# One-bank PSUM tiles for gate and up in the second token half of a fused attention and gated MLP kernel

## The chip, the cores and the metric

The kernel runs on one core of a Trainium2 chip. The metric is the device time of one launch in microseconds (us). The engines are named as in the profile: PE (TensorE, matmuls; PEld is its weight loads), DVE (VectorE), ACT (ScalarE), POOL (GpSimd) and SP (SyncE, which issues most transfers here).

## What is computed

The reference is a transformer block with adaptive layer norm: attention of 2048 tokens with 32 query heads over the last 512 cached keys, and then a gated MLP. The change touches the MLP only:

```
h = _layernorm(x) * (1 + cb) + sb          # [2048, 576]
gate = h @ W_gate                          # [2048, 4608]
up   = h @ W_up
gate = gate * (gate > 0)
x = x + gb * ((gate * up) @ W_down)        # [2048, 576]
```

All inputs are float32. The kernel splits a matmul operand into a high and a low part (`hi`, `lo`) and adds three products: hi with hi, hi with lo, lo with hi.

## The kernel before

**Order of the work.** On PE, DVE, ACT and POOL the instructions run in the order in which the program issues them; only SP's queue is ordered by the framework. Attention comes first (`NU` units), then the MLP, written as a generator (`mlp_slots`, L1412) that issues one *slot* at each step.

**Passes.** The MLP has 36 passes `m`. `m // NFP` (`NFP` = 18) is the token half, 1024 tokens as two blocks of 512, and `m % NFP` picks two of the 36 tiles of 128 features. A pass computes gate and up of a 2 x 2 block (two feature tiles by two token blocks) with seven products in place of eight, a scheme of Strassen's kind: `order` (L767) gives P1, P6, P2, P7, P5, P4, P3, and sums of the products make the four results. Passes 0 to 17 are the first token half, 18 to 35 the second.

**A slot** is one product. `prod` (L1034) runs 7 matmuls for the gate half (`xx` = 0) and 7 for the up half (`xx` = 1), each into 128 x 512 float32. P2 and P3 go on adding in the PSUM that P1 and P5 filled; the other five products get new PSUM from `new_pair` (L1147). In the second token half `evac_half` (L1098) is issued after each half: for gate it is one DVE instruction (L1074, L1076, L1110 or L1115, by product), for up one or two (L1079 adds into PSUM, L1080 multiplies the clipped gate with up; L1110; L1115, after which ACT copies the up half at L1117). P1 is the exception: nothing after the gate half, and one ACT copy of both halves (L1104) after the up half. Results are cut into hi and lo by ACT and POOL (`h_out`, `fast_split`).

**Pieces of the down projection** of pass m - 1 are put between the halves. An ordinary piece (`md_piece`, L647) is 12 matmuls into 128 x 576, which DVE adds to `acc` (L601). The passes in `FAST` (18 to 33) do the down projection too with seven products in place of eight: `fast_piece` (L659), 14 pieces of 6 matmuls, one in each half of the next pass's slots. Their sums are added to `acc` by DVE (L673, L679); in the first such pass, which starts the accumulators anew, eight of them are copied by ACT (L677). The weights for these pieces are made by POOL and ACT (`fast_weights`, L698), and operands by `fast_later` (L1082) and `fast_last` (L1092).

**PSUM.** A tile `[P, 2, 512]` float32 is a pair of banks, one for gate and one for up. The pool `psS` has two pairs, `psW` one; from the start of the MLP `psX` has one more, in the place of attention's `psM`. Gate and up take turns in three pairs, two of `psS` and the one of `psX`, by the list `free`: `new_banks` (L1142) takes its first entry, and L1446 puts a pair back when its last product is issued. All pieces use the one pair of `psW` (L584, L665), but for the last eight (L1450), of which every second one uses `psS`. The framework makes an instruction wait for earlier users of its tile.

**Loads.** `w_prep` (L828) loads the weights of the product two slots on (`wop`, 640 KB); it is called by `others` (L1404).

Of the kernel before, what the change touches and what calls it, by code (L numbers as in the profile page):

```python
# [7 lines left out]
F32 = mybir.dt.float32  # L8
# [3 lines left out]
ALU = mybir.AluOpType  # L12
AX = mybir.AxisListType

P = 128
# [16 lines left out]
def kernel(  # L32
# [13 lines left out]
    nc = tc.nc  # L46
# [11 lines left out]
    op = ctx.enter_context(tc.tile_pool(name="op", bufs=3))  # L58
    xp = ctx.enter_context(tc.tile_pool(name="xp", bufs=3))
    sp = ctx.enter_context(tc.tile_pool(name="sp", bufs=2))  # L60
    psS = ctx.enter_context(tc.tile_pool(name="psS", bufs=2, space=bass.MemoryType.PSUM))
    psW = ctx.enter_context(tc.tile_pool(name="psW", bufs=1, space=bass.MemoryType.PSUM))
    psM_scope = tc.tile_pool(name="psM", bufs=2, space=bass.MemoryType.PSUM)
    psM = psM_scope.__enter__()
# [576 lines left out]
    NFP = NFT // 2  # L641
    NB = 2 * NFP
    ds_, hhi, hlo = {}, {}, {}
    wop, wraw, hop = {}, {}, {}
    pair, tmp = {}, {}

    def md_piece(m, k, qt, pool=None):  # L647
        b, fp = divmod(m, NFP)
        i = 8 * b + 4 * k + qt
        down_piece([hhi[m, f, k] for f in range(2)], [hlo[m, f, k] for f in range(2)],  # L650
                   [ds_[m, f] for f in range(2)], i, qt, f"md{m}_{k}_{qt}", pool=pool)()
        if fp == NFP - 1:
            nc.sync.dma_start(out[i * P:(i + 1) * P, :], acc[i])


    FAST = range(NFP, NB - 2)
    fop, fw = {}, {}

    def fast_piece(m, kind, n):  # L659
        if kind == "4":  # L660
            specs = [(fop[m, "A22"], fw[m, "4"], 0, 2 * n + j) for j in range(2)]
        else:
            a, b = {"16": ("A11", "S2"), "75": ("S3", "S1"), "23": ("A12", "S4")}[kind]
            specs = [(fop[m, x], fw[m, kind], j * H2, n) for j, x in enumerate((a, b))]
        ps = psW.tile([P, 2, 512], F32, tag="w", name=f"mf{m}_{kind}_{n}")  # L665
        for j, ((hi, lo), (whi, wlo), c, qt) in enumerate(specs):
            sl = slice(qt * P, (qt + 1) * P)
            for i, (x, w) in enumerate(((hi, whi), (hi, wlo), (lo, whi))):
                nc.tensor.matmul(ps[:, j, :H2], x[:, sl], w[:, c:c + H2], start=i == 0, stop=i == 2)  # L669
        if kind == "4":  # L670
            for j in range(2):
                a = acc[8 + 2 * n + j][:, :H2]
                nc.vector.tensor_tensor(a, ps[:, j, :H2], a, op=ALU.add)  # L673
            return
        a = acc[{"16": 0, "75": 4, "23": 12}[kind] + n].rearrange("p (h n) -> p h n", h=2)
        if kind != "23" and m == FAST[0]:
            nc.scalar.copy(a, ps[:, :, :H2])  # L677
        else:
            nc.vector.tensor_tensor(a, ps[:, :, :H2], a, op=ALU.add)  # L679
# [87 lines left out]
    def order(m):  # L767
        return ("P1", "P6", "P2", "P7", "P5", "P4", "P3")
# [265 lines left out]
    def prod(m, s, n, xx):  # L1034

        hs, w = hop[m // NFP, OPS[s][1]], wop[n]
        ps = pair[m, s][:, xx, :]
        ops = []
        for t in range(2):
            ops += [(w[:, xx, t, :], hs[t]), (w[:, xx, 3 + t, :], hs[t]), (w[:, xx, t, :], hs[3 + t])]  # L1040
        ops.append((w[0:96, xx, 2, :], hs[2][0:96]))
        for i, (a, c) in enumerate(ops):
            nc.tensor.matmul(ps, a, c, start=s not in ("P2", "P3") and i == 0, stop=i == len(ops) - 1,  # L1043
                             skip_group_check=True)
# [26 lines left out]
    def gated_half(x, ps, r, a, op1=ALU.add):  # L1071
        if x == 0:
            if a is None:
                nc.vector.tensor_scalar(r, ps[:, 0, :], 0.0, None, op0=ALU.max)  # L1074
            else:
                nc.vector.tensor_tensor(r, ps[:, 0, :], a[:, 0, :], op=ALU.add)  # L1076
            return
        if a is not None:
            nc.vector.tensor_tensor(ps[:, 1, :], ps[:, 1, :], a[:, 1, :], op=op1)  # L1079
        nc.vector.scalar_tensor_tensor(r, r, 0.0, ps[:, 1, :], op0=ALU.max, op1=ALU.mult)  # L1080

    def fast_later(m):  # L1082
        r21, s1 = tmp[m, "r"][:, 0, :], tmp[m, "r"][:, 1, :]
# [8 lines left out]
    def fast_last(m):  # L1092
        r12, s4 = tmp[m, "q"][:, 0, :], tmp[m, "q"][:, 1, :]
        fast_split(m, "A12", r12)
        nc.gpsimd.tensor_sub(s4, r12, tmp[m, "c"][:, 1, :])
        fast_split(m, "S4", s4)

    def evac_half(m, s, x):  # L1098
        ps, fast = pair[m, s], m in FAST
        if s == "P1":  # L1100
            if x == 0:
                tmp[m, "q"] = pp.tile([P, 2, 512], F32, tag="hi", name=f"q{m}")
            else:
                nc.scalar.copy(tmp[m, "q"], ps)  # L1104
                if m - 1 in FAST:
                    fast_last(m - 1)
            return
        q = tmp[m, "q"]
        if s == "P6":
            nc.vector.tensor_tensor(q[:, x, :], ps[:, x, :], q[:, x, :], op=ALU.add)  # L1110
            return
        if s == "P7":
            if x == 0:
                tmp[m, "r"] = pp.tile([P, 2, 512], F32, tag="lo", name=f"r{m}", bufs=2)
            nc.vector.tensor_tensor(tmp[m, "r"][:, x, :], ps[:, x, :], q[:, x, :], op=ALU.add)  # L1115
            if x:
                nc.scalar.copy(q[:, 1, :], ps[:, 1, :])  # L1117
            return
        if s == "P2" and x == 0:
            tmp[m, "r22"] = xp.tile([P, 640], F32, tag="xm", name=f"r{m}")[:, :512]  # L1120
        if s == "P5" and x == 0:
            tmp[m, "c"] = pp.tile([P, 2, 512], F32, tag="lo", name=f"c22_{m}", bufs=2)
        f, k, r, a, op1 = {"P2": lambda: (0, 0, tmp[m, "r22"], None, ALU.add),
                           "P5": lambda: (1, 1, tmp[m, "c"][:, 0, :], tmp[m, "r"], ALU.add),
                           "P4": lambda: (1, 0, tmp[m, "r"][:, 0, :], tmp[m, "r"], ALU.add),
                           "P3": lambda: (0, 1, q[:, 0, :], q, ALU.subtract)}[s]()
        gated_half(x, ps, r, a, op1)
        if x == 0:
            return
        if not fast:  # L1130
            h_out(m, f, k, r)
        elif s == "P2":
            fast_split(m, "A22", r)
        elif s == "P5":
            fast_split(m, "A11", r)
        elif s == "P4":
            fast_later(m)


    npair, px, free, kind = [0], {}, ["s", "s"], {}  # L1140

    def new_banks(nm):  # L1142
        npair[0] += 1
        k = free.pop(0)
        return (px["x"] if k == "x" else psS).tile([P, 2, 512], F32, tag=k, name=nm), k

    def new_pair(m, s):  # L1147
        pair[m, s], kind[m, s] = new_banks(f"gu{npair[0]}")

    def evac(m, s):  # L1150
        ps = pair[m, s]
# [169 lines left out]
    for i in range(1, len(VIS)):  # L1321
        g, qbs = VIS[i]
# [40 lines left out]
    for i, ab in enumerate(lay0 + lay):  # L1363
        n = i - len(lay0) - 2 * NFT + 4
# [21 lines left out]
    for i in range(4):  # L1386
        m = 2 + 2 * i
# [23 lines left out]

    def mlp_slots():  # L1412
        for m in range(NB):
            md = [lambda k=k, qt=qt: md_piece(m - 1, k, qt) for k in range(2) for qt in range(4)] if m else []
            if m - 1 in FAST:
                md = fast_pieces(m - 1)
            for i, s in enumerate(order(m)):
                flush_stores()
                if s not in ("P2", "P3"):
                    new_pair(m, s)  # L1420
                else:
                    pair[m, s], kind[m, s] = (x[m, {"P2": "P1", "P3": "P5"}[s]] for x in (pair, kind))
                prod(m, s, 7 * m + i, 0)
                if m or i:
                    sums(m, i)
                    others(m, i)
                if m >= NFP:
                    evac_half(m, s, 0)
                if m and i or m - 1 in FAST:
                    md.pop(0)()  # L1430
                elif filler and not m:
                    filler.pop(0)()
                for fn in mextra.pop((m, i - 1, True), []):
                    fn()
                prod(m, s, 7 * m + i, 1)
                wop.pop(7 * m + i)
                if m >= NFP:
                    evac_half(m, s, 1)
                if m and i < 2 or m - 1 in FAST:
                    md.pop(0)()  # L1440
                elif filler and not i:
                    filler.pop(0)()
                if m < NFP:
                    evac(m, s)
                if s not in ("P1", "P5"):
                    free.append(kind[m, s])  # L1446
                yield
        for k in range(2):
            for qt in range(4):
                md_piece(NB - 1, k, qt, (psS, "s") if qt % 2 else None)  # L1450
        flush_stores()
        assert not mextra and not filler

# [202 lines left out]
```

## Time and profile before

| | us |
|---|---|
| median of 3 runs | 2997.86 (2995.13 to 2999.44) |
| the profiled execution | 2994.6 |
| its span, first to last instruction | 2992.5 |
| MLP, first token half: about | 1667 to 2323 |
| pass 18: about | 2323 to 2360 |
| pass 19 | 2360.55 to 2404.29 |
| passes 20 to 34 | 2404.29 to 2939.31 |
| pass 35 | 2939.31 to 2975.55 |
| the last eight pieces | 2975.55 to the end |

The page has the busy time of each engine, the chain of work that ended last, and the costliest groups of instructions. A row of a group reads: line, engine, operation, what is written from what, shape, count, then busy us and the mean ns of one, then the engine's idle time before them and who ended it. In the table of windows the columns are: the stretch, its length, busy us (and instructions) of PE, PEld, DVE, ACT and POOL, the granted TensorE clock, the DMA share, GB/s. In the list of waits the columns are us in total, times, longest us. A row in order of time gives the start, the duration, engine, line, what is done, the count of merged instructions, and in brackets the idle time before and its releaser.

### The profile page before, as it was taken

How to read it: one execution, taken by the hardware profiler on the slowest of the kernel's cores; microseconds unless marked ns; L12 is line 12 of the kernel's file. 1: busy time of each engine (PE TensorE's matmuls, PEld its weight loads, DVE VectorE, ACT ScalarE, POOL GpSimd, SP SyncE). 2: the span in 40 equal slices, each digit the busy share in tenths (PEclk: the TensorE clock that was granted, in tenths of full speed). 3: DMA queues.
4: the chain of work that ended last, by engine and by line, in shares of the span. 5: the costliest groups of instructions: out<-in, count | busy, mean ns of one | idle time of the engine just before them, and what ended most of it. 6: DMA issues, size and time to landing. Idle time of an engine off the chain costs nothing.

```text
span 2992.5 us, 41535 instructions
## 1 busy us (share of the span) xinstructions
PE 2900.6 (97%) x15256; PEld 2496.2 (83%) x15256; DVE 2189.5 (73%) x3058; ACT 1431.7 (48%) x1997; POOL 2195.5 (73%) x1597
## 2 busy tenths in 40 slices
PE   6799999999999999999999999999999899999999
PEld 5678888888888888888887888888888788888888
DVE  5778888888888888777889577767777355555555
ACT  4566666666676666666656333333323222222220
POOL 3767888888888888776777566677776466776773
PEclk8999999999999999999999999999999999999999
DMA  5322222222223323222243455666668644444443
GB/s 184 112 72 83 85 90 83 66 97 93 97 87 101 94 63 127 96 75 81 79 143 130 140 198 207 217 229 230 236 220 288 241 148 143 144 148 146 141 148 126
DMA packets 165898, 410.60 MB, mean 137 GB/s; under 512 B 15040, under 2 KB 61888, under 8 KB 165696
## 3 DMA queue, kind: packets, MB, share of 16 engines
q1 hardware_dynamic: 132944, 289.23, 30.0%
q10 hardware_dynamic: 32752, 118.73, 10.0%
q8 instruction: 121, 1.98, 0.3%
q14 instruction: 81, 0.66, 0.1%
HBM read 275.81 MB, written 160.40 MB: 146 GB/s over the span
## 4 chain that ended last, share of the span: by engine, by line
PE 85%; DVE 7%; POOL 3%; issue 2%; ACT 2%; DMA 2%; ACTq 0%; SPq 0%; DVEq 0%; POOLq 0%
PE gu L1043 25%; PE wo L590 13%; PE qps L387 12%; PE md L590 8%; PE mf L669 5%; PE s L463 3%; PE s L462 3%; PE s L461 3%; PE pv L565 3%; PE pv L564 3%; PE pv L563 3%; DVE wr L849 2%; POOL lo L545 1%; PE qm L489 1%; DVE t L466 1%
## 5 line engine op out<-in xcount | busy, mean ns | idle before, releaser
L545 POOL TENSOR_TENSOR lo<-p,hi 128x1024 fp32r<-128x1024 f32 x256 | 611.6, 2411 | 0.0
L554 POOL TENSOR_TENSOR ks<-ks,p 128x512 f32<-128x512 f32 x256 | 343.8, 1343 | 284.2 <-ACT p L538 210.5
L466 DVE TRANSPOSE_TENSOR_REDUCE t<-s 128x32 f32<-128x1024 f32 x256 | 316.3, 1243 | 134.5 <-PE s L463 123.4
L1043 PE MATMUL gu<-hop_B,wop 128*128 128x512 f32 (+1 forms) x1512 | 385.0, 398 | 0.4 <-DVE q L1076 0.2
L1043 PE MATMUL gu<-hop_T,wop 128*128 128x512 f32 (+1 forms) x1260 | 327.2, 399 | 5.3 <-DMA wop<-wk_P 1.9
L1043 PEld LDWEIGHTS gu<-hop_B,wop 128*128 128x128 f32 (+1 forms) x1512 | 277.1, 190 | 60.7 <-DVE q L1076 3.8
L536 DVE TENSOR_TENSOR p<-s,mb 128x1024 f32<-128x1024 f32 x250 | 295.2, 1219 | 4.2
L387 PE MATMUL qps<-hTa,wA 128*128 128x512 f32 x1176 | 284.8, 393 | 6.6 <-ACT wA L185 4.1
L590 PE MATMUL wo<-woga,ohi 128*128 128x288 f32 x1344 | 280.4, 302 | 0.0
L590 PE MATMUL md<-wogb,hhi 128*128 128x288 f32 x1280 | 263.9, 299 | 15.6 <-DVE acc L601 15.6
L1043 PEld LDWEIGHTS gu<-hop_T,wop 128*128 128x128 f32 (+1 forms) x1260 | 227.4, 189 | 59.8 <-DVE q L1110 5.3
L538 ACT ACTIVATE p<-p 128x1024 f32<-128x1024 f32 x250 | 264.0, 1056 | 17.7 <-DVE p L536 15.8
L525 ACT CAST hi<-p 128x1024 fp32r<-128x1024 f32 x256 | 269.0, 1051 | 7.0
L387 PEld LDWEIGHTS qps<-hTa,wA 128*128 128x128 f32 x1176 | 222.5, 190 | 55.3 <-ACT wA L185 4.5
L590 PEld LDWEIGHTS md<-wogb,hhi 128*128 128x128 f32 x1280 | 214.5, 190 | 31.1 <-DVE acc L601 20.2
L441 ACT ACTIVATE qhi<-qps 128x512 fp32r<-128x512 f32 x128 | 76.5, 597 | 341.8 <-PE qps L387 341.8
L601 DVE TENSOR_TENSOR acc<-md,acc 128x576 f32<-128x576 f32 x160 | 120.8, 755 | 145.3 <-PE md L590 144.2
L590 PEld LDWEIGHTS wo<-woga,ohi 128*128 128x128 f32 x1344 | 218.9, 189 | 6.6
L590 PE MATMUL wo<-woga,olo 128*128 128x288 f32 x672 | 198.8, 296 | 0.4 <-POOL olo L579 0.2
L590 PE MATMUL md<-wogb,hlo 128*128 128x288 f32 x640 | 190.1, 297 | 0.0
L599 ACT COPY acc<-wo 128x576 f32<-128x576 f32 x232 | 147.6, 636 | 69.0 <-PE wo L590 65.1
L579 POOL TENSOR_TENSOR olo<-rb,ohi 128x512 fp32r<-128x512 f32 x128 | 167.2, 1307 | 17.1 <-ACT ohi L575 17.0
(271 smaller groups left out, 7263.2 us busy)
## 6 DMA issues: line engine op xcount, KB each, us to landing
wop<-wk_P SPq DMA_DIRECT2D x133, 640.0 KB
wk_P<-wop ACTq DMA_DIRECT2D x119, 640.0 KB
wr<-wlay SPq DMA_DIRECT2D x68, 384.0 KB
againq<-akq SPq DMA_DIRECT2D x22, 640.0 KB
againo<-ako SPq DMA_DIRECT2D x18, 576.0 KB
rogb<-wd SPq DMA_DIRECT2D x36, 288.0 KB
rwA<-wq SPq DMA_DIRECT2D x32, 320.0 KB
wlay<-wg SPq DMA_DIRECT2D x36, 256.0 KB
```

The costliest lines, as they stand in the source:

```text
L387: return [lambda i=i, a=a, b=b: nc.tensor.matmul(ps, a, b, start=(i == 0), stop=(i == n - 1)) for i, (a, b) in enumerate(ops)]
L466: nc.vector.tensor_reduce(t4[u][:, 2 * h:2 * h + 2, :].rearrange("p k b -> p (k b)"), t.rearrange("p k (b j) -> p (k b) j", j=32), axis=AX ...
L525: nc.scalar.copy(hi_[u, h], pt[u, h])
L536: nc.vector.tensor_tensor(p, t, bc[u][:, None, :].to_broadcast([P, 2, 512]), op=ALU.subtract)
L538: nc.scalar.activation(p, p, AF.Exp, bias=0.0, scale=1.0)
L545: nc.gpsimd.tensor_sub(lo_[u, h], pt[u, h], hi_[u, h].bitcast(F32))
L554: nc.gpsimd.tensor_tensor(ks_[u], ks_[u], p[:, j, :], op=ALU.add)
L579: nc.gpsimd.tensor_sub(olo[u], o.pop(u), ohi[u].bitcast(F32))
L590: nc.tensor.matmul(ps[:, half, :H2], a[:, sl], w[b][:, cs], start=(n == 0 and seed is None), stop=(n == 5), skip_group_check=seed is not None)
L599: nc.scalar.copy(av, ps[:, :, :H2])
L669: nc.tensor.matmul(ps[:, j, :H2], x[:, sl], w[:, c:c + H2], start=i == 0, stop=i == 2)
L1043: nc.tensor.matmul(ps, a, c, start=s not in ("P2", "P3") and i == 0, stop=i == len(ops) - 1, skip_group_check=True)
```

## The change

For passes 18 to 35, gate and up of a product get a tile of one bank each. The pool `psS` is closed when pass 18 starts, and a pool `psG` opens in its place, with two names, `a` and `b`, of two one-bank tiles each. Which name a product takes follows from the product and from whether the pass is even or odd. The pair of `psX` no longer serves gate and up; from pass 19 on the pieces of the down projection take it and the pair of `psW` in turn, the last eight too. P1's copy is made in two halves, one after each half of the product. `psS` is allocated from the other side of PSUM, so that it can be closed before `psX`. What is multiplied and added stays the same.

```
-    psS = ctx.enter_context(tc.tile_pool(name="psS", bufs=2, space=bass.MemoryType.PSUM))
+    psS_scope = tc.tile_pool(name="psS", bufs=2, space=bass.MemoryType.PSUM, side="right")
+    psS = psS_scope.__enter__()
...
     def fast_piece(m, kind, n):
...
-        ps = psW.tile([P, 2, 512], F32, tag="w", name=f"mf{m}_{kind}_{n}")
+        pool = md_pool()
+        ps = pool[0].tile([P, 2, 512], F32, tag=pool[1], name=f"mf{m}_{kind}_{n}")
...
     def prod(m, s, n, xx):
...
-        ps = pair[m, s][:, xx, :]
+        ps = pair[m, s][:, xx, :] if m < NFP else pair[m, s][xx]
...
     def evac_half(m, s, x):
-        ps, fast = pair[m, s], m in FAST
+        ps, fast = pair[m, s][x], m in FAST
         if s == "P1":
             if x == 0:
                 tmp[m, "q"] = pp.tile([P, 2, 512], F32, tag="hi", name=f"q{m}")
-            else:
-                nc.scalar.copy(tmp[m, "q"], ps)
-                if m - 1 in FAST:
-                    fast_last(m - 1)
+            nc.scalar.copy(tmp[m, "q"][:, x, :], ps)
+            if x and m - 1 in FAST:
+                fast_last(m - 1)
             return
...
+    def open_g():
+        psS_scope.__exit__(None, None, None)
+        px["g"] = ctx.enter_context(tc.tile_pool(name="psG", bufs=2, space=bass.MemoryType.PSUM, side="right",
+                                                 reuse_waits="tile"))
+
+    def md_pool():
+        px["n"] = px.get("n", 0) + 1
+        return (px["x"], "x") if px["n"] % 2 else (psW, "w")
+
...
     def new_pair(m, s):
-        pair[m, s], kind[m, s] = new_banks(f"gu{npair[0]}")
+        if m < NFP:
+            pair[m, s], kind[m, s] = new_banks(f"gu{npair[0]}")
+            return
+        if "g" not in px:
+            open_g()
+        kind[m, s] = "ab"[(s in ("P6", "P7", "P4")) ^ m % 2]
+        pair[m, s] = [px["g"].tile([P, 512], F32, tag=kind[m, s], name=f"gh{m}_{s}_{i}") for i in range(2)]
...
     def mlp_slots():
         for m in range(NB):
-            md = [lambda k=k, qt=qt: md_piece(m - 1, k, qt) for k in range(2) for qt in range(4)] if m else []
+            md = [lambda k=k, qt=qt: md_piece(m - 1, k, qt, md_pool() if m > NFP else None)
+                  for k in range(2) for qt in range(4)] if m else []
...
-                if s not in ("P1", "P5"):
+                if s not in ("P1", "P5") and m < NFP:
                     free.append(kind[m, s])
                 yield
         for k in range(2):
             for qt in range(4):
-                md_piece(NB - 1, k, qt, (psS, "s") if qt % 2 else None)
+                md_piece(NB - 1, k, qt, md_pool())
```

In `gated_half` and the rest of `evac_half`, `ps[:, x, :]` becomes `ps`, which is now the tile of that half.

More of the change, by code (lines that the diff above doesn't have):

```diff
@@ L1073, in gated_half @@
             if a is None:
-                nc.vector.tensor_scalar(r, ps[:, 0, :], 0.0, None, op0=ALU.max)
+                nc.vector.tensor_scalar(r, ps, 0.0, None, op0=ALU.max)
             else:
-                nc.vector.tensor_tensor(r, ps[:, 0, :], a[:, 0, :], op=ALU.add)
+                nc.vector.tensor_tensor(r, ps, a[:, 0, :], op=ALU.add)
             return
         if a is not None:
-            nc.vector.tensor_tensor(ps[:, 1, :], ps[:, 1, :], a[:, 1, :], op=op1)
-        nc.vector.scalar_tensor_tensor(r, r, 0.0, ps[:, 1, :], op0=ALU.max, op1=ALU.mult)
+            nc.vector.tensor_tensor(ps, ps, a[:, 1, :], op=op1)
+        nc.vector.scalar_tensor_tensor(r, r, 0.0, ps, op0=ALU.max, op1=ALU.mult)
     def fast_later(m):
@@ L1109, in evac_half @@
         if s == "P6":
-            nc.vector.tensor_tensor(q[:, x, :], ps[:, x, :], q[:, x, :], op=ALU.add)
+            nc.vector.tensor_tensor(q[:, x, :], ps, q[:, x, :], op=ALU.add)
             return
@@ L1114, in evac_half @@
                 tmp[m, "r"] = pp.tile([P, 2, 512], F32, tag="lo", name=f"r{m}", bufs=2)
-            nc.vector.tensor_tensor(tmp[m, "r"][:, x, :], ps[:, x, :], q[:, x, :], op=ALU.add)
+            nc.vector.tensor_tensor(tmp[m, "r"][:, x, :], ps, q[:, x, :], op=ALU.add)
             if x:
-                nc.scalar.copy(q[:, 1, :], ps[:, 1, :])
+                nc.scalar.copy(q[:, 1, :], ps)
             return
```

## The prediction

> **What bounds the kernel now.** I read the page first, for the busy shares and the chain of work that ended last.
>
> ```profile
> PE 2900.6 (97%) x15256; PEld 2496.2 (83%) x15256; DVE 2189.5 (73%) x3058; ACT 1431.7 (48%) x1997; POOL 2195.5 (73%) x1597
> L1043 PEld LDWEIGHTS gu<-hop_B,wop 128*128 128x128 f32 (+1 forms) x1512 | 277.1, 190 | 60.7 <-DVE q L1076 3.8
> ```
>
> TensorE (PE) is busy 97% of the span, so only idle time of PE, or work taken from it, can pay. The change takes no matmul away. The second row is the first hint: weight loads of the gate and up products were held up by DVE evacuations (L1076).
>
> Next the table of windows. A pass (m) has seven products; a product with its pieces of the down projection is a slot, and a slot has two halves, gate and up, each 7 matmuls and, in passes 19 to 34, one piece of 6. The rows are passes of the first token half, pass 19, passes 20 to 34 together, pass 35.
>
> ```profile
> 2266.75:2311.67 44.92, 44.92 (x247) 39.71 (x247) 29.29 (x33) 13.03 (x18) 29.04 (x27) 1.00 0.86 302
> 2360.55:2404.29 43.74, 37.69 (x183) 30.76 (x182) 14.62 (x23) 14.47 (x25) 31.43 (x28) 0.96 0.42 138
> 2404.29:2939.31 535.02, 532.64 (x2733) 443.18 (x2731) 312.79 (x466) 115.58 (x192) 365.08 (x308) 1.00 0.45 148
> 2939.31:2975.55 36.24, 35.75 (x197) 31.24 (x196) 21.50 (x32) 4.09 (x6) 17.34 (x18) 1.00 0.22 71
> ```
>
> Passes 20 to 34 take 535.02 / 15 = 35.67 us each. PE looks nearly full there (532.64 of 535.02), but its matmul rows are pipelined and hide short stops. What a slot costs without stops is in the chain that ended last, in the first token half, where the same 14 + 12 matmuls make a slot:
>
> ```profile
> 2302.04 3.22 PE gu L1043 x14
> ...
> 2311.67 3.22 PE gu L1043 x14
> ```
>
> These are the first and the third of three slots in a row: (2311.67 − 2302.04) / 2 = 4.815 us a slot, 33.7 us for seven. So a pass of the second half loses 35.67 − 33.70 = 1.97 us. Where, say the waits of weight loads in passes 20 to 34:
>
> ```profile
> PEld mf L669 <- DVE acc L679: 6.7, 30, 0.3
> PEld gu L1043 <- DVE q L1110: 4.4, 15, 0.3
> PEld gu L1043 <- DVE r L1115: 4.3, 15, 0.3
> PEld gu L1043 <- DVE c L1076: 4.1, 15, 0.3
> PEld mf L669 <- ACT fh_A L695: 3.6, 14, 0.3
> PEld gu L1043 <- DVE r L1074: 3.3, 15, 0.2
> PEld gu L1043 <- DVE q L1076: 3.1, 15, 0.2
> PEld gu L1043 <- DVE r L1076: 1.4, 9, 0.2
> ```
>
> Together 30.9 us, 2.06 a pass: nearly all that is missing, and no transfer is among them. L1110, L1115, L1074 and L1076 read the gate half of a product; the loads that wait belong to its up half. One place in order of time (start, duration; P6 gate, its evacuation, P6 up, P2 gate):
>
> ```profile
> 2444.83 1.47 PEld L1043 LDWEIGHTS gu<-hop_T,wop 128*128 128x128 f32 x7
> 2446.85 0.69 DVE L1110 TENSOR_TENSOR q<-gu,q 128x512 f32<-128x512 f32 x1 [0.86 <-PE gu L1043]
> 2447.59 1.45 PEld L1043 LDWEIGHTS gu<-hop_T,wop 128*128 128x128 f32 x7 [0.29 <-DVE q L1110]
> 2449.99 1.48 PEld L1043 LDWEIGHTS gu<-hop_B,wop 128*128 128x128 f32 x7
> ```
>
> The gate half takes 2.76 us, the up half 2.40. The up product writes the other half of the same tile and uses nothing that L1110 makes; it waits because the tile is handed over as one. P1, the only product whose gate half is not evacuated at once, is the only one whose up product has no such wait.
>
> **The change, part by part.** *Four one-bank tiles instead of pairs.* Gate and up have tiles of their own, so six waits a pass go: (4.4 + 4.3 + 4.1 + 3.3 + 3.1 + 1.4) / 15 = 1.37 us. *Two pairs for the pieces.* They have one pair now (L665), so a piece waits until the last was added to acc. The 30 waits on L679 and the 14 put down to L695 are that: where L695 is named, the addition before it ended at the same moment, as these rows show (up product of P5, its two evacuations, the addition, the cast, the next piece, and last the up product of P3):
>
> ```profile
> 2463.02 1.89 PE L1043 MATMUL gu<-hop_T,wop 128*128 128x512 f32 x7
> 2464.94 0.70 DVE L1079 TENSOR_TENSOR gu<-gu,r 128x512 f32<-128x512 f32 x1 [1.17 <-PE gu L1043]
> 2465.68 0.69 DVE L1080 SCALAR_TENSOR_TENSOR c<-c,gu 128x512 f32<-128x512 f32 x1
> 2466.28 0.75 DVE L679 TENSOR_TENSOR acc<-mf,acc 128x576 f32<-128x576 f32 x1
> 2466.40 0.62 ACT L695 CAST fh_A<-c 128x512 fp32r<-128x512 f32 x1 [4.34 <-DVE c L1080]
> 2467.15 0.30 PEld L669 LDWEIGHTS mf<-fw,fh_A 128*128 128x128 f32 x2 [0.25 <-ACT fh_A L695]
> ...
> 2473.23 1.46 PEld L1043 LDWEIGHTS gu<-hop_B,wop 128*128 128x128 f32 x7 [0.21 <-DVE q L1076]
> ```
>
> The addition ends at 2467.03, the cast at 2467.02. With two pairs a piece needs the one before the last, which is some 2.4 us older; the three waits a pass, (6.7 + 3.6) / 15 = 0.69 us, go too. All of it is bounded by the floor, so I count 1.97 us a pass and not 2.06: **15 × 1.97 = 29.5 us** (30.9 by the waits).
>
> *What it costs: gate and up keep two pairs instead of three.* The names alternate from slot to slot (a b a b a b a, next pass b a b a b a b), so a bank is written again two slots later. For the up bank of P5: product from 2463.02, last read by L1080, done at 2466.37; P3 writes it next at 2473.23, without the stops 2 × 4.815 = 9.63 us after 2463.02, at 2472.65. That leaves 6.3 us, and this is the longest evacuation (two instructions, and L1117 on ACT for P7 is shorter). No wait is added that is not over long before. The accumulations P1 to P2 and P5 to P3 stay in their banks as before.
>
> *P1's copy in two halves.* One L1104 becomes two of L1117's form:
>
> ```profile
> L1104 ACT COPY q<-gu 128x1024 f32<-128x1024 f32 x14 | 14.2, 1015 | 51.6 <-PE gu L1043 51.6
> L1117 ACT COPY q<-gu 128x512 f32<-128x512 f32 x15 | 8.7, 582 | 8.8 <-DVE r L1115 8.8
> ```
>
> 2 × 0.58 − 1.02 = 0.15 us more of ACT a pass, on an engine busy 115.58 of 535.02 us: nothing. Queued behind the first half copy is only the second, and the casts of fast_last after it start 0.4 us earlier. *DVE, POOL and the transfers* get 33.7 us for the work of 35.67: DVE 312.79 / 505.5 = 62%, POOL 72%, the DMA share 0.45 becomes 0.48; none is near full. The order of the loads on SP is not written out in the kernel and could come out otherwise; no PE wait in these passes is on a load, so I cost it at nothing.
>
> *Pass 19* loses more, 43.74 − 33.70 = 10.0 us, for it starts the accumulators with copies on ACT (L677), which stand behind casts that wait for a late POOL:
>
> ```profile
> 2368.91 0.19 PEld L669 LDWEIGHTS mf<-fw,fp_S 128*128 128x128 f32 x1 [1.17 <-POOL fp_S L696]
> 2369.97 1.46 PEld L1043 LDWEIGHTS gu<-hop_T,wop 128*128 128x128 f32 x7 [0.87 <-DVE q L1110]
> 2373.82 0.62 ACT L695 CAST fh_S<-q 128x512 fp32r<-128x512 f32 x1 [4.11 <-POOL q L1095]
> 2374.92 0.63 ACT L677 COPY acc<-mf 128x576 f32<-128x576 f32 x1
> 2375.60 0.50 PEld L669 LDWEIGHTS mf<-fw,fh_A 128*128 128x128 f32 x2 [4.17 <-ACT acc L677]
> 2380.54 1.45 PEld L1043 LDWEIGHTS gu<-hop_B,wop 128*128 128x128 f32 x7 [0.22 <-DVE r L1074]
> 2386.91 0.43 ACT L727 CAST fqhi<-fu 128x288 fp32r<-128x288 f32 x1 [2.52 <-POOL fu L722]
> 2387.25 0.63 ACT L677 COPY acc<-mf 128x576 f32<-128x576 f32 x1
> ```
>
> The wait of 1.17 us on POOL stays. Then the up product of P6 starts at 2369.3, the next piece needs no copy, P2's gate product follows at 2371.8, and only the piece after it waits for the copy that ends at 2375.55: P2's up product starts at 2376.5 instead of 2380.54. POOL is in arrears and does not come forward, so some is given back: the copy of 2387.25 stands behind the cast that waits for fu; I estimate its end as 2386.9 instead of 2387.88, since POOL's chain before it waits less for ACT. The piece that needs its pair is due at 2376.5 + 3 × 2.41 + 1.5 = 2385.2 and waits 1.7 us. From there the up product of P5 and five halves more, 0.9 + 5 × 2.41, end the pass near 2399.9 instead of 2404.29: **4.4 us** less. Bounds: 0, if POOL sets all, and 10.0, if all goes.
>
> *Pass 35* has two waits, in front of the up products of P4 and P3, where DVE is late:
>
> ```profile
> 2968.71 1.46 PEld L1043 LDWEIGHTS gu<-hop_T,wop 128*128 128x128 f32 x7 [0.48 <-DVE r L1076]
> 2974.05 1.46 PEld L1043 LDWEIGHTS gu<-hop_B,wop 128*128 128x128 f32 x7 [0.48 <-DVE q L1076]
> ```
>
> With the start of the pipeline 0.54 us each, **1.1 us**. *Pass 18* stops for weights in its third product anyway:
>
> ```profile
> 2341.36 1.46 PEld L1043 LDWEIGHTS gu<-hop_T,wop 128*128 128x128 f32 x7 [2.33 <-DMA wop<-wk_P]
> ```
>
> What is saved before is waited for there, and a wait of up to 2.33 us at the change of pools would be hidden by it: nothing. Uncovered it would cost those 2.33 us. The last eight pieces keep two pairs or more, and so their time.
>
> **Sum:** 29.5 + 4.4 + 1.1 = **35.0 us**. The profiled execution took 2994.6 us (span 2992.5) and would take 2959.6. It lies 3.3 us under the median of the runs, 2997.86; from that, **2962.9 us**.
>
> **The rivals.** *Only one part works.* If the tiles' waits go and the pieces' stay, 1.37 / 2.06 of 29.5, and 1.1, and some 1 of pass 19: 21.7 us, 2976. If only the pieces' go, 9.9 + 3: 2985. For it: one DVE queue answers for both, and a wait taken away can show up in the next one. Against: DVE is idle before most of these evacuations (0.86 and 1.17 us above). *Nothing moves*: the up product really waits for DVE's order, not the tile, and 2998 stays. Against stands P1. [...]
>
> *The two pairs do not alternate* (slower). If a slot got the banks that the slot just before it used, and got them as a pair, its gate product would wait for the evacuations of the up product before it. These end 3.35 us after that product starts (2463.02 to 2466.37), and the next half starts after 2.41 us: 0.94 us lost for P5, P4 and P3, 0.2 for P2 and P6 (one instruction of 0.69 us), 0.8 for P7 (L1115, then L1117). That is 4.0 us a pass, 60 in all: 2963 + 60 = 3023. It decides from 35 / 15 = 2.3 us a pass. The order of the names speaks against it.
>
> *The granted clock falls* as PE loses its pauses. In pass 19 the row above has 0.96; at that, 505.5 us become 526.6, and 2984 results; at 0.935 all is lost. Against: the first row of windows has PE without a pause at 1.00. [...]
>
> **How the numbers follow.** The forecast has 0.82; one part only 0.08; nothing 0.04; not alternating 0.03; clock 0.03. The forecast's own range: pass 19 from 0 to 10.0 instead of 4.4, 30.9 instead of 29.5, about 3 us for where the runs fall: 2953 to 2970. To 2978 it takes in the likelier half of the first rival. 0.2% is 6 us, about what a measurement of this kernel can tell from no change: faster 0.82 + 0.08 + 0.03 = 0.93, same 0.04, slower 0.03.
>
> **What would show it.** In the profile after, passes 20 to 34 are 33.7 us apart; no weight load of gu waits for L1110, L1115, L1074 or L1076, and none of mf for L679; pass 19 is near 39.3 us and still shows POOL; PEclk stays 1.00. A wait of gu on L1080 or L1117 would mean that two pairs are too few; one on wop, that a load came late; passes of 34.4 us, that only the tiles paid.

## The result, and the profile after

The changed kernel takes 2960.98 us (median of 4 runs, 2957.22 to 2964.77), the kernel before 2996.49 us (4 runs on the same chip, 2991.03 to 2999.44): a ratio of 0.9884, with a 95% interval of 0.9864 to 0.9903. The change makes the kernel 35.5 us faster (29 to 41 by the interval); forecast were 35.0. The profiled execution took 2957.2 us, its span is 2955.4.

On the page, TensorE's own busy time has shrunk with the span and the share stays 97%; the granted clock is 9 tenths or more from the second slice on; and what holds up the weight loads of the new tiles (`gh_P`) most is a transfer, no longer VectorE:

```profile
PE 2871.7 (97%) x15256; PEld 2496.5 (84%) x15256; DVE 2184.3 (74%) x3058; ACT 1434.2 (49%) x2015; POOL 2196.4 (74%) x1597
PEclk8999999999999999999999999999999999999999
L1045 PEld LDWEIGHTS gh_P<-hop_T,wop 128*128 128x128 f32 (+1 forms) x1008 | 181.4, 188 | 33.2 <-DMA wop<-wk_P 1.7
```

The stretches follow in the table of windows: pass 19, passes 20 to 34, pass 35, the last eight pieces (each cut at the first weight load of P1, as before; columns as before).

```profile
2356.91:2396.11 39.20, 35.94 (x184) 30.73 (x183) 14.69 (x23) 14.03 (x26) 31.13 (x27) 0.96 0.46 154
2396.11:2903.33 507.22, 507.22 (x2733) 443.84 (x2731) 312.68 (x466) 118.22 (x208) 365.66 (x308) 1.00 0.47 157
2903.33:2938.50 35.17, 35.17 (x197) 31.17 (x195) 21.43 (x32) 4.25 (x7) 17.69 (x18) 1.00 0.23 73
2938.50:2955.40 16.90, 13.14 (x98) 12.86 (x96) 7.45 (x10) 0.62 (x1) 1.29 (x1) 1.00 0.37 141
```

Passes 20 to 34 went from 535.02 to 507.22 us, 27.8 less, 33.81 us a pass. Pass 19 lost 43.74 − 39.20 = 4.5 us, pass 35 36.24 − 35.17 = 1.1. That is 33.4 us. The span is 37.1 us shorter. Of the rest, 3.0 us lie ahead of the changed passes: pass 18's first weight load comes at 2319.97 where it came at 2323.01, behind work that is the same (its scatter is taken up at the end). Another 0.6 us are pass 18's own (36.94 us instead of 37.54): its third product waits 1.7 us for a load where it waited 2.3.

All waits of weight loads from 2300 us to the end, well over a hundred before:

```profile
PEld mf L671 <- ACT acc L679: 2.8, 1, 2.8
PEld gh_P L1045 <- DMA wop<-wk_P: 1.7, 1, 1.7
PEld mf L671 <- POOL fp_S L698: 1.2, 1, 1.2
```

None is left in passes 20 to 34. One place there in order of time, P7's gate half, a piece, the evacuation of the gate half, and P7's up half:

```profile
2410.61 1.47 PEld L1045 LDWEIGHTS gh_P<-hop_T,wop 128*128 128x128 f32 x7
2412.12 0.95 PEld L671 LDWEIGHTS mf<-fw,fp_S 128*128 128x128 f32 x6
2412.61 0.69 DVE L1116 TENSOR_TENSOR r<-gh_P,q 128x512 f32<-128x512 f32 x1 [0.92 <-POOL ft L717]
2413.02 1.48 PEld L1045 LDWEIGHTS gh_P<-hop_T,wop 128*128 128x128 f32 x7
```

The evacuation runs from 2412.61 to 2413.30, and the up half's loads begin at 2413.02, in the midst of it. In the kernel before they came after it. The halves are 2413.02 − 2410.61 = 2.41 us apart (2.76 in the place shown of before).

### The profile page after: what moved, and what is told of

The parts are those of the page before. It is cut to its first block, busy times and chain, and to the rows that moved or that the text cites. A ratio compares the mean times of both kernels' runs of the same rounds, so it can differ in the third digit from the quotient of the medians.

```text
span 2955.4 us, 41574 instructions
## 1 busy us (share of the span) xinstructions
PE 2871.7 (97%) x15256; PEld 2496.5 (84%) x15256; DVE 2184.3 (74%) x3058; ACT 1434.2 (49%) x2015; POOL 2196.4 (74%) x1597
## 4 chain that ended last, share of the span: by engine, by line
PE 85%; DVE 6%; POOL 3%; ACT 2%; DMA 2%; issue 2%; SPq 0%; ACTq 0%; DVEq 0%; POOLq 0%
PE gh_P L1045 13%; PE wo L591 13%; PE qps L388 12%; PE gu L1045 11%; PE md L591 8%; PE mf L671 6%; PE s L464 3%; PE s L463 3%; PE s L462 3%; PE pv L566 3%; PE pv L565 3%; PE pv L564 3%; DVE wr L851 2%; POOL lo L546 1%; PE qm L490 1%
## 5 line engine op out<-in xcount | busy, mean ns | idle before, releaser
L1045 PE MATMUL gh_P<-hop_T,wop 128*128 128x512 f32 (+1 forms) x1008 | 255.8, 393 | 1.3 <-DMA wop<-wk_P 1.3
L591 PEld LDWEIGHTS md<-wogb,hhi 128*128 128x128 f32 x1280 | 214.2, 189 | 29.5 <-DVE acc L602 18.6
L1045 PEld LDWEIGHTS gh_P<-hop_T,wop 128*128 128x128 f32 (+1 forms) x1008 | 181.4, 188 | 33.2 <-DMA wop<-wk_P 1.7
L1045 PE MATMUL gh_P<-hop_B,wop 128*128 128x512 f32 (+1 forms) x756 | 192.7, 395 | 0.0
L1045 PE MATMUL gu<-hop_B,wop 128*128 128x512 f32 (+1 forms) x756 | 187.4, 394 | 0.0
```

The source lines that it names most:

```text
L591: nc.tensor.matmul(ps[:, half, :H2], a[:, sl], w[b][:, cs], start=(n == 0 and seed is None), stop=(n == 5), skip_group_check=seed is not None)
```

## The experiments

Each edit is made in the changed kernel. In its numbering the evacuation of P6 is L1111, that of P7 L1116 (in the second experiment each stands one line lower), L1074 and L1076 have become L1076 and L1078, L677 and L679 have become L679 and L681, and the rows of pieces stand at L671. The kernel before ran beside them on the same chips: 2994.99 us (15 runs) beside the first four, 2993.83 (7 runs) beside the next four, 2994.41 (9 runs) beside the last.

### The tiles alone

```
     def md_pool():
         px["n"] = px.get("n", 0) + 1
-        return (px["x"], "x") if px["n"] % 2 else (psW, "w")
+        return psW, "w"
```

Gate and up keep their one-bank tiles; all pieces use the one pair of `psW`, the last eight too.

> The changed kernel, but all pieces of the down projection in passes 19 to 35 use the one pair of psW again; gate and up keep their one-bank tiles. Theory (two separate sources that add: six tile waits of 1.37 us and three piece waits of 0.69 us a pass before): the piece waits come back and the tile waits do not. Passes 20 to 34 take 33.81 + 1.86 x 0.69 / 2.06 = 34.4 us instead of 33.81; weight loads of mf wait for L679's addition about three times a pass, none of gh_P for a gate evacuation; pass 19 is back near 43 us, for the copies on ACT hold the one pair. Time 2961 + 9 + 4 = 2974. Rival A (one DVE queue answers for both, and what one wait gives the other takes): passes near 35.5 us and 2990. Rival B (the pieces' second pair does nothing): 33.8 us and 2961.

It took 2977.14 us (2973.48 to 2979.18), a ratio of 0.9937 (0.9925 to 0.995). Its windows (pass 19, passes 20 to 34, pass 35 with the last eight pieces) and then its waits in passes 20 to 34:

```profile
2360.76:2403.78 43.02, 36.37 (x183) 30.57 (x182) 14.81 (x23) 14.36 (x26) 31.18 (x26) 0.96 0.40 140
2403.78:2914.25 510.47, 510.47 (x2733) 440.38 (x2731) 312.74 (x466) 118.02 (x207) 365.11 (x309) 1.00 0.46 156
2914.25:2974.13 59.88, 50.03 (x292) 44.15 (x290) 28.76 (x42) 4.87 (x8) 18.71 (x19) 0.99 0.23 83
```

```profile
PEld mf L671 <- DVE acc L681: 6.8, 30, 0.3
PEld mf L671 <- ACT fh_A L697: 3.8, 14, 0.3
```

The waits on evacuations are gone and those of the pieces stand as they did (6.7 and 3.6 before). But a pass takes 510.47 / 15 = 34.03 us, not 34.4: the tiles alone bring 24.55 of the 27.8 us. Pass 19 hardly moves (43.02), so its gain is the pieces'. The last row shows a second thing: pass 35 and the last eight pieces together are 59.88 us, against 35.17 + 16.90 = 52.07 in the changed kernel. One pair for the last pieces costs 7.8 us, with six waits of 1.1 us on the additions among them; that is half of what this kernel is slower.

### The pieces alone

```
...
-        pair[m, s] = [px["g"].tile([P, 512], F32, tag=kind[m, s], name=f"gh{m}_{s}_{i}") for i in range(2)]
+        t = px["g"].tile([P, 2, 512], F32, tag=kind[m, s], name=f"gh{m}_{s}", bufs=1)
+        whole[m, s] = t
+        pair[m, s] = [t[:, i, :] for i in range(2)]
...
```

Two tiles of two banks for gate and up, and P1 copied whole, as before; the pieces keep their two pairs. `psG` keeps its setting `reuse_waits="tile"`, which `psS` lacks, so what this kernel loses is not owed to that setting. In pass 18 VectorE copies P7's up half, since ScalarE's queue stands behind the last pieces of pass 17 there.

> The changed kernel, but a product's gate and up are again the two halves of one two-bank tile, handed over as one (P1 with one copy after its up half, as before); the pieces keep their two pairs. In pass 18 alone the copy of P7's up half is made by DVE in place of ACT. Theory (the tile is handed over as one, and that is what the up product waits for): the six waits of a pass come back, passes 20 to 34 take 33.81 + 1.86 x 1.37 / 2.06 = 35.05 us; loads of the gate and up products wait for L1110, L1115, L1074 and L1076, none of mf for an addition; pass 35 gets its 1.1 us back. Time 2961 + 18.6 + 1.1 + 1 = 2982. Rival A (one DVE queue): near 35.5 us and 2990. Rival C (the up product waited for DVE's order, not for the tile; the second pair of the pieces freed it): 33.8 us and 2961.

It took 2988.95 us, a ratio of 0.9981 (0.9972 to 0.999). Pass 19 and passes 20 to 34, then the waits in the latter:

```profile
2361.04:2400.46 39.42, 35.75 (x184) 29.64 (x183) 14.68 (x23) 13.59 (x24) 31.35 (x28) 1.00 0.45 154
2400.46:2934.83 534.37, 531.31 (x2733) 447.30 (x2732) 312.66 (x466) 115.67 (x192) 364.53 (x309) 1.00 0.44 149
```

```profile
PEld gh_P L1045 <- DVE q L1112: 4.7, 15, 0.6
PEld gh_P L1045 <- DVE r L1117: 4.7, 15, 0.7
PEld gh_P L1045 <- DVE c L1078: 4.1, 15, 0.3
PEld gh_P L1045 <- DVE q L1078: 3.3, 15, 0.2
PEld gh_P L1045 <- DVE r L1076: 3.3, 15, 0.2
PEld gh_P L1045 <- DVE r L1078: 3.3, 15, 0.2
```

Pass 19 has nearly all of its gain (43.74 to 39.42), the steady passes have none to speak of: 534.37 / 15 = 35.62 us where 35.67 were and 35.05 were expected. 10.3 us of pieces' waits went, and the time fell by 0.65. The six waits on evacuations add up to 23.4 us; in the kernel before they were 20.6. So part of what the piece no longer waits for, the up half behind it waits for longer. All of these waits stand in front of an up half, none in front of a gate half: that there are two pairs instead of three costs nothing here.

The two experiments give prices for recorded waits. Here 23.4 us of waits in front of products stand for 534.37 − 507.22 = 27.15 us of time. With the tiles alone, 10.6 us of waits in front of pieces stand for 510.47 − 507.22 = 3.25 us: 0.3 us of time for each us recorded. The 2.8 us (23.4 less 20.6) by which the up halves wait longer without the pieces' waits thus come to about as much as these 3.25 us, and so the second pair of the pieces brings next to nothing by itself. Single places of the kernel before agree: P6's gate half, with 0.29 us of a product's wait behind it, takes 2.76 us; P1's gate half, from 2439.93 to 2442.42 with 0.26 us of a piece's wait in it, takes 2.49; without a wait it is 2.41. Why a piece's wait is so cheap was not shown. Two places of the kernel before differ in the order of ends and starts, though the ends of matmuls are modelled: in the first pair of rows a product's matmuls of 512 columns end at 2441.83, after the piece's load has begun at 2441.66; in the second a piece's of 288 end at 2447.54, before the up product begins at 2447.59.

```profile
2440.06 1.77 PE L1043 MATMUL gu<-hop_B,wop 128*128 128x512 f32 x7
2441.66 0.19 PEld L669 LDWEIGHTS mf<-fqhi,fh_A 128*128 128x128 f32 x1 [0.26 <-DVE acc L679]
...
2446.98 0.56 PE L669 MATMUL mf<-fw,fp_S 128*128 128x288 f32 x3
2447.59 1.89 PE L1043 MATMUL gu<-hop_T,wop 128*128 128x512 f32 x7
```

### The names in another order, and P1's copy late

```
-        kind[m, s] = "ab"[(s in ("P6", "P7", "P4")) ^ m % 2]
+        kind[m, s] = "ab"[s in ("P6", "P4")]
```

P2 goes on in P1's banks and P3 in P5's, so P7 now takes the banks that P2 has just used, P5 those of P7, and the next pass's P1 those of P3. In pass 18 VectorE copies P7's up half, as above.

> The changed kernel, but the names of the tiles do not alternate: P6 and P4 take b, all others a, so that P7, P5 and the next pass's P1 get the banks that the slot just before them used. In pass 18 alone the copy of P7's up half is made by DVE in place of ACT. Theory (with one-bank tiles each bank is free when its own reader is done): the up bank is written again 4.83 us after the up product before it started, and its evacuation is done 2.6 us (P2), 3.2 us (P7) or 3.35 us (P3) after it, so nothing waits: passes 33.8 us, time 2961 within 4. The prediction's slower rival (a slot that gets the last slot's banks waits for their evacuation): 0.2 + 0.8 + 0.9 = 1.9 us a pass, passes 35.7 us, time 2961 + 30 = 2991.

```
-            nc.scalar.copy(tmp[m, "q"][:, x, :], ps)
-            if x and m - 1 in FAST:
-                fast_last(m - 1)
+            if x:
+                for j in range(2):
+                    nc.scalar.copy(tmp[m, "q"][:, j, :], pair[m, s][j])
+                if m - 1 in FAST:
+                    fast_last(m - 1)
```

> The changed kernel, but both half copies of P1 come after its up half. Theory (the copy in halves is hidden): passes 33.8 us, no new wait, P6's gate evacuation some 0.5 us later. Rival (the earlier half copy is part of the gain, since P6's evacuation and fast_last wait for it): 0.3 us a pass more, passes 34.1 us, waits of gh_P on L1105 or L1112.

They took 2960.4 us (2957.68 to 2961.76; ratio 0.9879, 0.9864 to 0.9894) and 2963.8 (one run). Passes 20 to 34 in the first and in the second:

```profile
2400.78:2907.98 507.20, 507.20 (x2732) 443.86 (x2731) 312.72 (x466) 118.19 (x207) 364.94 (x309) 1.00 0.46 157
```

```profile
2402.76:2909.98 507.22, 507.22 (x2733) 444.15 (x2731) 312.74 (x466) 118.05 (x207) 365.43 (x309) 1.00 0.46 157
```

Both are the changed kernel's 507.22 to 0.02 us. The slower rival falls: with tiles of one bank, even the less favourable order leaves no wait. And P1's half copies are hidden, early or late, as forecast.

### Pass 19 and the first token half

What holds pass 19 at 39.2 us? In order of time, of the changed kernel:

```profile
2370.24 0.62 ACT L697 CAST fh_S<-q 128x512 fp32r<-128x512 f32 x1 [4.11 <-POOL q L1097]
2371.34 1.17 ACT L679 COPY acc<-mf 128x576 f32<-128x576 f32 x2
2372.02 0.30 PEld L671 LDWEIGHTS mf<-fw,fh_A 128*128 128x128 f32 x2 [2.76 <-ACT acc L679]
2372.79 2.37 PEld L1045 LDWEIGHTS gh_P<-hop_B,wop 128*128 128x128 f32 x7
```

ScalarE waits for GpSimd, casts, and only then copies the first sums that TensorE waits for. Behind it, seven loads take 2.37 us in place of 1.48. Four kernels try this and the first half's waits: the changed kernel again, one with the first edit below, one with the second, one with both.

```
-            nc.scalar.copy(a, ps[:, :, :H2])
+            nc.vector.tensor_copy(a, ps[:, :, :H2])
```

```
         for m in range(NB):
-            md = [lambda k=k, qt=qt: md_piece(m - 1, k, qt, md_pool() if m > NFP else None)
+            if m == 9:
+                free.remove("x")
+            md = [lambda k=k, qt=qt: md_piece(m - 1, k, qt, md_pool() if m > 8 else None)
```

> The changed kernel once more, beside the next three. 2961 us, within 4 either way; passes 20 to 34 at 33.8 us each, pass 19 at about 39.2 us, with TensorE's waits of pass 19 on ScalarE's first sums (one or two of 1.7 to 2.8 us) and on GpSimd's cast (about 1.2 us).

> The first sums of pass 19 are written by VectorE instead of ScalarE, nothing else. If the excess of pass 19 over a steady pass (39.2 against 33.8 us) comes mainly of TensorE's waiting for ScalarE to give a pair of banks back, the wait on the first sums (2.8 us in the profile of the changed kernel) goes, and with it the stretch of slower loads behind it (0.9 us in one group of seven); GpSimd's 1.2 us stays: pass 19 at about 35.5 us, the whole about 4 us below the changed kernel, 2957 us. If pass 19 is held by GpSimd and the order of its pieces instead, a wait of the same length comes up elsewhere: pass 19 at 38 us or more, and the whole within 1 us of the changed kernel.

> From pass 9 on in the first token half, one of the three pairs of banks leaves the ring of the gate and up products, which keeps two whole pairs, and the pieces of the down projection alternate between that pair and their own. If the waits of the first half's pieces on VectorE's sums (13.5 us in all in the profile of the changed kernel, 8 of them) are paid in full, as pass 19's were, they go: about 2948 us. If two whole pairs are too few for the gate and up products, as a product's tile then comes round after one other product instead of two, TensorE waits for the evacuations instead: up to 1.9 us a pass over nine passes, so 2961 to 2965 us, and the waits stand on the gate and up tiles.

> The two edits before together. They touch different stretches (the first half's passes from 9 on, and pass 19), so their gains should add: 2944 us if both hold, 2957 if only the first does, 2948 if only the second does.

| | median us (range) | ratio to before |
|---|---|---|
| the changed kernel again | 2960.99 (2956.51 to 2962.75) | 0.9886 (0.9869 to 0.9902) |
| first sums by VectorE | 2960.38 (2960.34 to 2960.72) | 0.9889 (0.9874 to 0.9904) |
| two pairs for pieces from pass 9 | 2951.16 (2946.5 to 2954.03) | 0.9856 (0.9842 to 0.9871) |
| both | 2944.66 (2940.17 to 2946.54) | 0.9834 (0.9819 to 0.9849) |

*The first sums.* Pass 19 in the changed kernel again, and in the kernel with the first edit:

```profile
2362.59:2401.74 39.15, 34.59 (x183) 29.44 (x182) 14.81 (x23) 13.97 (x26) 31.16 (x26) 1.00 0.44 153
```

```profile
2364.38:2399.40 35.02, 34.08 (x184) 29.62 (x183) 20.70 (x31) 9.46 (x18) 31.20 (x26) 1.00 0.49 173
```

The pass loses 4.1 us (3.7 were expected); the 1.2 us that remain above 33.81 are GpSimd's wait. So pass 19 was held by ScalarE's order, and the first branch of the expectation holds for the pass. Yet the medians differ by 0.6 us only. In the profiles pass 19 starts 1.8 us later with the edit (2364.38 against 2362.59), by code that the edit does not touch, and so the spans differ by 2.3. The whole time by itself doesn't show this edit; the pass does. With both edits, the pass is 35.02 us again, and there the median is 6.5 us below that of the second edit alone.

*The first half.* From pass 9 to the end of pass 17, in the changed kernel, in its second profile, and with the second edit:

```profile
1986.97:2320.20 333.23, 322.86 (x1747) 283.27 (x1747) 242.92 (x241) 106.16 (x151) 252.34 (x216) 0.99 0.70 249
```

```profile
1986.43:2322.90 336.47, 325.05 (x1747) 284.50 (x1747) 247.84 (x241) 106.03 (x151) 252.60 (x216) 0.98 0.69 246
```

```profile
1987.25:2315.05 327.80, 321.26 (x1746) 281.54 (x1747) 249.64 (x244) 106.45 (x151) 254.88 (x216) 0.99 0.71 256
```

The waits of weight loads in that stretch (those under 0.5 us in all left out), first of the changed kernel, then with the second edit:

```profile
PEld md L591 <- DVE acc L602: 13.5, 8, 4.0
```

```profile
PEld gu L1045 <- issue: 5.8, 4, 3.5
PEld gh_P L1045 <- DVE q L1070: 2.7, 1, 2.7
PEld gu L1045 <- ACT q L1178: 0.9, 2, 0.5
```

The pieces' waits (13.5 us) are gone, and the median falls by 9.8 us, not by 13. Some comes back: 2.7 us at the seam, where a one-bank tile of pass 18 takes a bank that the first half's evacuation (L1070) still reads, 0.9 us on ScalarE's copies of a product's up half (L1178), since two whole pairs are now and then too few, and 5.8 us that the profile puts down to no releaser. With both edits the kernel takes 2944.66 us, as the sum had it (2944). That is in part luck: measured one by one the edits brought 0.6 and 9.8 us, and 5.9 us more came with both. It is 16.3 us below the changed kernel, the best but for the next, which can't be told from it.

### Both pieces of a slot together

```
-                if m and i or m - 1 in FAST:
+                if m and i and m - 1 not in FAST:
                     md.pop(0)()
...
-                if m and i < 2 or m - 1 in FAST:
+                if m and i < 2 and m - 1 not in FAST:
+                    md.pop(0)()
+                elif m - 1 in FAST:
+                    md.pop(0)()
                     md.pop(0)()
```

> The two edits of the kernel before this one, and from pass 19 on both pieces of a slot stand behind the product's second half instead of one behind each half, so that TensorE goes over between the two kinds of work twice a slot instead of four times. If the 0.11 us by which the changed kernel's steady pass (33.81 us) misses the forecast floor (33.70) is the price of going over between the kinds, passes 20 to 34 come to 33.70 us, and the whole to 2943 us against the 2944.7 of the kernel with the two edits alone. If it is a price of the one-bank tiles or of the pieces' two pairs, the passes stay at 33.81 us. Should a wait on gate or up banks come back because both halves of the next product now follow at once, the passes rise to 34 us or more.

It took 2943.53 us (2940.08 to 2946.59; ratio 0.983, 0.9816 to 0.9844). Pass 19 and passes 20 to 34:

```profile
2344.86:2379.23 34.37, 34.08 (x184) 29.54 (x183) 20.29 (x32) 9.94 (x19) 32.00 (x27) 1.00 0.50 179
2379.23:2885.93 506.70, 506.70 (x2733) 444.29 (x2732) 307.74 (x467) 117.46 (x207) 365.39 (x309) 1.00 0.46 157
```

506.70 / 15 = 33.78 us a pass: going over between the kinds of work half as often saves 0.03 us, not 0.11. Most of what the forecast floor misses is something else, and stays open. Pass 19 gains a further 0.65 us: a piece now stands later, and GpSimd's wait of 1.2 us is gone. In its place one wait on a bank came back, 0.7 us in front of a product, on ScalarE's copy of P7's up half:

```profile
PEld gh_P L1045 <- ACT q L1118: 0.7, 1, 0.7
```

## Why the prediction was right, step by step

**What bounds the kernel, and the floor.** Right. A slot without stops was put at 4.815 us, a pass at 33.70; the passes measure 33.81. 0.11 us a pass, 1.6 in all, is the miss. The stretches named in the forecast gained 33.4 us; that the medians differ by 35.5, so near to 35.0, is luck within their scatter.

**Where the waits come from.** Right. The up half waited for the gate half's evacuation because of the tile: with the tile split, the wait is gone although the evacuation runs at the same place; with the tile whole again and all else changed, it is back (23.4 us).

**How the 1.97 us a pass divide.** The sum was right (27.8 us for 29.5), the division wrong. The step that failed is reading each part's share off its own rows of waits: 1.37 for the tiles and 0.69 for the pieces. Alone, the tiles bring 24.55 / 15 = 1.64, the pieces 0.65 / 15 = 0.04. The sum held since it was bounded by the floor, not by the waits; the rival "only one part works", made of the same shares, was mispriced for that reason: by the steady passes the tiles alone leave 3.25 us of the gain behind, the pieces alone 27.15.

**Two pairs are enough for gate and up.** Right: no wait on L1082 or on P7's copy, and none with the names in a worse order. In pass 18 it was luck. ScalarE's queue stands there behind the last pieces of pass 17 (17.96 us idle), and it copies P7's up half only at 2356.06, after P4's up product, which the alternation would put into the same bank, has begun (2350.66). In the program as built, P4's up half of this one pass lies in the bank of P4's gate half instead, and nothing waits; the prediction had not looked at this.

**P1's copy, the other engines, the loads:** nothing, as forecast. The one load waited for after 2300 us (1.7 us) is in pass 18, where one of 2.33 was; in the second profile it is 3.1 us.

**Pass 19.** 4.4 us forecast, 4.5 measured; GpSimd's 1.17 us and one wait for ScalarE's copy are there as described. The second wait, estimated at 1.7 us, isn't in this profile. In its place is a stretch at a granted clock of 0.50: 2369.80 to 2373.20 is the stop, 2373.20 to 2376.60 what follows.

```profile
2369.80:2373.20 3.40, 1.18 (x8) 1.14 (x9) 0.62 (x1) 2.92 (x6) 2.67 (x3) 1.00 0.14 57
2373.20:2376.60 3.40, 3.40 (x11) 2.83 (x10) 0.68 (x1) 0.56 (x1) 3.40 (x4) 0.50 0.00 0
```

There the loads of P2's up half begin at 2372.79, those of the piece behind it at 2375.25 and the next product's at 2376.76: 3.97 us, where P7's gate half and its piece, shown above, take 2.41. These 1.56 us come to about the same as the 1.7. In the second profile the clock of pass 19 is 1.00 (its row above), and the pass takes 39.15 us with both waits for ScalarE, of 2.8 and 4.5 − 2.8 = 1.7 us, as estimated:

```profile
PEld mf L671 <- ACT acc L679: 4.5, 2, 2.8
```

**Pass 35** lost 1.1 us, **the last eight pieces** nothing, as forecast. That the last pieces need their second pair was said there in passing; it is worth 7.8 us. **Pass 18**, put at nothing, lost 0.6.

**The rivals.** "Nothing moves" and "the clock falls" are refuted by 33.81 us a pass at a clock of 1.00: where evacuations held TensorE, one-bank tiles alone paid 24.55 us. "They do not alternate" is refuted by the order of names tried above: it supposed tiles handed over as pairs, and one-bank tiles aren't.

## What to carry to other kernels

Where two products go into one PSUM tile and one of them is evacuated while the other is computed, look for short waits of weight loads (here 0.2 to 0.3 us each, 84 of them) on that evacuation: a tile for each bank took them away with no more PSUM. Bound the gain by the time of a stretch that runs without stops, not by adding up waits, since here the waits in front of pieces cost 0.3 us for each us recorded (3.25 for 10.6), and those in front of products 1.2 (27.15 for 23.4). And look at the passes at the seams (pass 19, the last pieces, the first half's) by themselves: the pieces' second pair of banks was worth 0.2 us a pass in the steady state (3.25 us in fifteen passes), and 4 to 10 us in each of these.

## What the runs showed of the hardware

In pass 5 both the second profile of the changed kernel and the profile of the kernel with the first sums by VectorE have the same wait of 2.5 us, by unchanged code, and the pass takes 37.66 us in the one and 39.13 in the other: 1.47 us more, over half of the wait. The whole pass, and in it two stretches of 3.41 us, the stop and what follows; first of the former, then of the latter:

```profile
1837.61:1875.27 37.66, 35.55 (x196) 31.15 (x195) 29.94 (x27) 11.05 (x16) 22.48 (x21) 1.00 0.54 202
...
1870.59:1874.00 3.41, 2.05 (x14) 2.01 (x15) 3.34 (x6) 0.02 (x1) 1.77 (x1) 1.00 0.38 142
1874.00:1877.41 3.41, 3.41 (x17) 2.77 (x16) 3.31 (x8) 1.45 (x2) 2.73 (x3) 1.00 0.64 250
```

```profile
1838.09:1877.22 39.13, 37.03 (x196) 32.24 (x194) 31.33 (x31) 11.50 (x16) 23.95 (x23) 0.96 0.58 208
...
1870.59:1874.00 3.41, 1.57 (x12) 1.57 (x13) 3.34 (x5) 0.00 (x0) 2.24 (x2) 1.00 0.54 214
1874.00:1877.41 3.41, 3.41 (x11) 2.74 (x10) 3.34 (x8) 1.45 (x2) 2.25 (x3) 0.50 0.67 250
```

In the latter the stop came 0.5 us later (the load behind it begins at 1872.43 in place of 1871.95); TensorE was busy 1.57 us of the first stretch in place of 2.05, and the second has a granted clock of 0.50: 11 matmuls in place of 17. In pass 19 of the first profile of the changed kernel, a stretch with TensorE busy 1.18 of 3.40 us is followed by one at 0.50 too (its rows above). Why the clock is 0.50 behind the one stop and 1.00 behind the other was not shown.

So unchanged code scatters. The latter profile is 1.95 us behind at the end of pass 5 (1877.22 against 1875.27) and 1.79 at the start of pass 19 (2364.38 against 2362.59). In the profiles of kernels with the same first half and no wait in passes 20 to 34, these passes repeat to 0.03 us (507.19 to 507.22), and the start of pass 19 lies anywhere from 2356.9 to 2364.4 us. An edit that moves a few us in one place is better read from its own pass than from the whole time.
